# A mixture of experts' second product for both column halves ahead of most outputs

## The chip, the cores and the metric

The kernel runs on one core of a Trainium2 chip. That core has five engines with instruction streams of their own: PE (TensorE, matrix products; its weight loads are shown as PEld), DVE (VectorE), ACT (ScalarE), POOL (GpSimd) and SP (SyncE, which here issues all transfers). Sixteen transfer engines (DMA) move data between the chip's memory and the core. The metric is the device time of one execution, in microseconds (us). The kernel before takes 621.01 us, the median of three runs (620.48 to 622.41).

## The reference

Attention with a learned bias, whose output is the input x of a soft mixture of experts. Batch B = 8, 8 heads, sequence 576, head size 64; so x has 8 x 576 = 4608 rows of 512. There are 8 experts with 4 slots each (32 slots) and a hidden size of 1024. The expert part is:

```python
logits = x @ phi                                   # 4608 x 32
d = softmax over the rows of logits
slot_input = d.T @ x                               # 32 x 512
for e in range(8):
    h = np.maximum(slot_input[e] @ w1[e], 0.0)     # 4 x 1024
    slot_out[e] = h @ w2[e]                        # 4 x 512
c = softmax over the slots of logits               # 4608 x 32, the combine weights
return c @ slot_out                                # 4608 x 512
```

The matrices w1 and w2 have 512 x 1024 and 1024 x 512 numbers per expert, in fp32. All that follows from `slot_input` on needs every row of x, as the first softmax runs over all rows.

## The kernel before

**The long part.** Some 545 of the 620 us go to attention, in 32 units of two heads and one batch, and to the logits and slot inputs of the batches. Its order is written out by hand, in the table `END` (line 42) and in `PLAIN`, and it ends at line 820. The change leaves it as it is. Behind line 820 the order on each engine is chosen by a planner that goes by the order of the program text as priority, puts later work that is ready by its own estimates into an engine's gaps, and adds all waits. Each engine then runs its list strictly in that order.

**Weights.** `fetch_w` (line 755) loads one tile of 512 KB per call: 32 tiles of w1, then 32 of w2, in the list `worder` (line 745). A tile of w2 is one expert, half of the hidden size (`fq`) and half of the 512 output columns (`hf`). The list goes by column half first: 16 tiles of column half 0, then 16 of column half 1, and within a half by expert group `Q` (four experts each), `fq`, and expert `g`. 41 of the 64 tiles are asked for in the hand-ordered part, into every buffer that comes free there; the others follow in the loop of the first product (lines 862 to 884), each into the buffer of a w1 tile that the loop has used, and two behind it (line 886). All of them go through SP's queue.

**First product.** The loop over j = 0 to 7 (lines 862 to 884) takes expert group Q = j // 4 and a quarter kc of the 512 inputs. The eight matmuls of one j put four experts side by side on PE (L867). After four j the result passes a ReLU on ACT into `hS2[Q]` (L881). `turn_hidden(Q)` (line 854) turns these rows with 8 PE transposes (L858) and two copies into `hT2[Q]`, as the second product needs them. Both calls use PSUM tile 3.

**Turned combine weights.** `stack(b)` (line 835) prepares batch b's combine weights for the last matmul: DVE splits them into a rounded part and its remainder (L839, L840), PE turns both (five transposes, L844 and L845, in PSUM tile 2), and ACT or DVE copies 128 x 576 numbers into `cst` (line 846). One `stack` stands in each of the eight turns of the loop.

**Second product.** Lines 893 to 939 run once per column half `hf`. The 64 matmuls of a half (L900, two instructions each in the trace) sum over the hidden size for both expert groups. The loop goes over `Q`, `fq`, then a quarter `x` of the tile, and innermost over the four experts' tiles `g`. DVE and ACT copy the sums to `so` (L905); two matmuls with the selection matrices `sel` fold the experts' rows together (L908); ACT and DVE write `sst`, again a rounded part and its remainder (L910, L911).

**Outputs.** For each of eight batches, four matmuls (L930) give 512 rows of 256 columns; two copies of 128 x 512 (`ld.copy`, lines 114 and 120) bring them to a buffer `ob`, and one transfer of 512 KB stores it in rows of 4 KB (L933). The last 64 of the 576 rows take one more matmul per batch (L936) and a copy per two batches into `obr`, stored for four batches at once, 256 KB in pieces of 1 KB from 64 partitions (L939). `ld.copy` (line 109) chooses ACT or DVE by a running estimate of their load. `ps(k)` is a PSUM tile of two banks, with k = 0 to 3; a new use of one waits for the last one's end.

Of the kernel before, what the change touches and what calls it, by code (L numbers as in the profile page):

```python
# [10 lines left out]
F32 = mybir.dt.float32  # L11
F32R = mybir.dt.float32r
AF = mybir.ActivationFunctionType
ALU = mybir.AluOpType
# [111 lines left out]
def body(ctx, tc, qk, v, wcol, phi, mw1, mw2, tabh, consth, out):  # L126
    nc = tc.nc
    P = 128
    S, D = 576, 64
    B, NP = qk.shape[0:2]  # L130
    H = 2 * NP
    NSL = phi.shape[1]
    E, DM, F = mw1.shape
# [6 lines left out]
    wp = ctx.enter_context(tc.tile_pool(name="wp", bufs=W1N))  # L140
    ldp = ctx.enter_context(tc.tile_pool(name="ldp", bufs=2))
    bsp = ctx.enter_context(tc.tile_pool(name="bsp", bufs=5))
    yp = ctx.enter_context(tc.tile_pool(name="yp", bufs=4))
    atp = ctx.enter_context(tc.tile_pool(name="atp", bufs=1))
    xp = ctx.enter_context(tc.tile_pool(name="xp", bufs=1))
    smp = ctx.enter_context(tc.tile_pool(name="smp", bufs=4))

    ld = Split(nc)

    def ps(k):  # L150

        return psp.tile([P, 2, 512], F32, name="ps", tag=f"r{k}")
# [165 lines left out]
    for i, x in enumerate(END.split()):  # L318
        n, u = x.rstrip("+").split("/")
# [490 lines left out]
    homes = {21: (bsp, "bm"), 22: (ldp, "qk"), 27: (ldp, "qk"), 32: (atp, "at0"), 34: (atp, "at1"), 36: (xp, "xk")}  # L810
# [21 lines left out]
        nc.vector.tensor_scalar(out=sel[Q], in0=rsum, scalar1=rowm[:, Q:Q + 1], scalar2=None, op0=ALU.mult)  # L832
    csts = [bsp.tile([P, S], F32R, name="cst", tag="br", bufs=1)]

    def stack(b):
        cst = csts[b]
        cs = xp.tile([P, 5, 2, 2, 32], F32R, name="cs", tag=("acc", "et")[b % 2])
        ckb = ck[:, b].unsqueeze(2).to_broadcast([P, 5, 2, 32])
        nc.vector.tensor_copy(out=cs[:, :, :, 0, :], in_=ckb)  # L839
        nc.vector.tensor_tensor(out=cs[:, :, :, 1, :], in0=ckb, in1=cs[:, :, :, 0, :].bitcast(F32), op=ALU.subtract)  # L840
        csf = cs.bitcast(F32).rearrange("a c x y s -> a c (x y s)")
        pt = ps(2).rearrange("a x n -> a (x n)")
        for c in range(4):
            nc.tensor.transpose(out=pt[:, c * P:(c + 1) * P], in_=csf[:, c, :], identity=ident)  # L844
        nc.tensor.transpose(out=pt[:, 512:576], in_=csf[0:64, 4, :], identity=ident[0:64, 0:64])  # L845
        ld.copy(cst, pt[:, 0:576], 576)
# [3 lines left out]
    def hidden():  # L850
        hS2.append(wp.tile([P, 2, 512], F32, name="hS", tag="w"))
        hT2.append(wp.tile([P, 8, P], F32, name="hT", tag="w"))

    def turn_hidden(Q):
        pt = ps(3)
        for z in range(2):
            for x in range(4):
                nc.tensor.transpose(out=pt[:, z, x * P:(x + 1) * P], in_=hS2[Q][:, z, x * P:(x + 1) * P], identity=ident)  # L858
            ld.copy(hT2[Q][:, 4 * z:4 * z + 4, :], pt[:, z].rearrange("a (x n) -> a x n", x=4), 512)

    ph = None
    for j in range(8):
        Q, kc = j // 4, j % 4
        ph = ps(Q) if kc == 0 else ph
        for n in range(2):
            for g in range(4):
                nc.tensor.matmul(ph[32 * g:32 * g + 32, n, :], sT[:, kc, :], wtiles[4 * j + g][n],  # L867
                                 start=kc == 0, stop=kc == 3, tile_position=(0, 32 * g))

        if j == 0:  # L870
            csts.append(wp.tile([P, S], F32R, name="cst", tag="w"))
        elif j in (1, 2):
            csts += [wp.tile([P, S], F32R, name="cst", tag="w") for _ in range(2)]
        elif j in (3, 4):
            csts.append(wp.tile([P, S], F32R, name="cst", tag="w"))
            hidden()
        for i in range(4 * j + (1, 2, 2, 3, 3, 0, 0, 0)[j], 4 * j + 4):
            if nw[0] < len(worder):
                fetch_w(homeof[i])
        if kc == 3:  # L880
            nc.scalar.activation(out=hS2[Q], in_=ph, func=AF.Relu, scale=stS)  # L881
        if j == 4:
            turn_hidden(0)
        stack(j)
    turn_hidden(1)
    while nw[0] < len(worder):
        fetch_w((wp, "w"))
    wi = 32


    so = wp.tile([P, 2, 512], F32, name="so", tag="w")
    sstt = wp.tile([P, DM], F32R, name="sst", tag="w")
    for hf in range(2):
        ds = slice(256 * hf, 256 * hf + 256)
        po = ps(3)[:, 0].rearrange("a (x n) -> a x n", x=2)
        for Q in range(2):
            for fq in range(2):
                for x in range(4):
                    for g in range(4):
                        nc.tensor.matmul(po[32 * g:32 * g + 32, Q, :], hT2[Q][:, 4 * fq + x, 32 * g:32 * g + 32],  # L900
                                         wtiles[wi + g][x // 2][:, 256 * (x % 2):256 * (x % 2) + 256], start=fq == 0 and x == 0,
                                         stop=fq == 1 and x == 3, tile_position=(0, 32 * g))
                wi += 4
        for Q in range(2):
            (nc.scalar.copy if Q else nc.vector.tensor_copy)(out=so[:, hf, 256 * Q:256 * Q + 256], in_=po[:, Q, :])  # L905
        pf = ps(2)[:, 0]
        for Q in range(2):
            nc.tensor.matmul(pf[:, 0:256], sel[Q], so[:, hf, 256 * Q:256 * Q + 256], start=Q == 0, stop=Q == 1)  # L908
        sst = sstt[:, ds]
        nc.scalar.copy(out=sst, in_=pf[:, 0:256])  # L910
        nc.vector.tensor_tensor(out=sst[64:], in0=pf[64:, 0:256], in1=sst[64:].bitcast(F32), op=ALU.subtract)  # L911
        ld.act = ld.dve = 0.0
        for bq in range(2):
            obr = wp.tile([P, 4, 256], F32, name="obr", tag="w")
            for i in range(4):
                b = 4 * bq + i
                cst = csts[b]
                if hf == 1:
                    ob = (yp, bsp)[bq].tile([P, 4, 256], F32, name="ob", tag=("y", "bm")[bq])
                elif b > 3:  # L920
                    ob = wp.tile([P, 4, 256], F32, name="ob", tag="w")
                elif b % 2 == 0:
                    pool, tag = ((atp, "at0"), (xp, "xk"))[b // 2]
                    obs = pool.tile([P, 2, 4, 256], F32, name="ob", tag=tag)
                    ob = obs[:, 0]
                else:
                    ob = obs[:, 1]
                po = ps(b % 2).rearrange("a x (y n) -> a (x y) n", y=2)
                for c in range(4):
                    nc.tensor.matmul(po[:, c, :], cst[:, c * P:(c + 1) * P], sst, start=True, stop=True)  # L930
                for z in range(2):
                    ld.copy(ob[:, 2 * z:2 * z + 2, :], po[:, 2 * z:2 * z + 2, :], 512)
                nc.sync.dma_start(out=out[b, hf, :, 0:1024], in_=ob.rearrange("p c d -> p (c d)"))  # L933
                if i % 2 == 0:
                    pr = ps(2).rearrange("a x (y n) -> a (x y) n", y=2)
                nc.tensor.matmul(pr[0:64, i % 2, :], cst[:, 512:576], sst, start=True, stop=True)  # L936
                if i % 2 == 1:
                    ld.copy(obr[0:64, i - 1:i + 1, :], pr[0:64, 0:2], 512)
            nc.sync.dma_start(out=out[4 * bq:4 * bq + 4, hf, 0:64, 1024:1280].rearrange("b p d -> p b d"), in_=obr[0:64])  # L939


def _tables():
# [54 lines left out]
```

## Time and profile before

| | |
|---|---|
| median of three runs | 621.01 us (620.48 to 622.41) |
| profiled execution | 621.36 us, its span 619.6 us |
| busy: PE, DVE, ACT, POOL | 95%, 68%, 77%, 36% of the span |
| transfers | 110.72 MB, mean 179 GB/s |
| L867, first product | 128 instructions, 548.6 to 569.8 us |
| L900, second product | 256 instructions, first from 575.2, last from 598.6 us |
| L933 and L939, outputs | 20 issues, from 588.1 to 613.2 us; 9.44 MB |

All times within the execution count from the start of the span. An engine's busy share is an average over stages that have different limits, so the part around the change has to be read on its own. In the views of time windows, the columns are busy us of PE, PEld, DVE, ACT and POOL with the number of instructions, the mean granted TensorE clock (1.00 is full speed), the mean busy share of the transfer engines (overlapping packets can bring it above 1) and GB/s.

### The profile page before, as it was taken

How to read it: one execution, taken by the hardware profiler on the slowest of the kernel's cores; microseconds unless marked ns; L12 is line 12 of the kernel's file. 1: busy time of each engine (PE TensorE's matmuls, PEld its weight loads, DVE VectorE, ACT ScalarE, POOL GpSimd, SP SyncE). 2: the span in 40 equal slices, each digit the busy share in tenths (PEclk: the TensorE clock that was granted, in tenths of full speed). 3: DMA queues.
4: the chain of work that ended last, by engine and by line, in shares of the span. 5: the costliest groups of instructions: out<-in, count | busy, mean ns of one | idle time of the engine just before them, and what ended most of it. 6: DMA issues, size and time to landing. Idle time of an engine off the chain costs nothing.

```text
span 619.6 us, 18796 instructions
## 1 busy us (share of the span) xinstructions
PE 591.4 (95%) x7359; PEld 378.6 (61%) x7359; DVE 422.6 (68%) x1339; ACT 474.0 (77%) x979; POOL 223.9 (36%) x336
## 2 busy tenths in 40 slices
PE   6998899999999999999999999999999999999882
PEld 3764566666666666666666666666656666544452
DVE  7997766666666766666667666686788887664143
ACT  6997788888888888888888888787886877532242
POOL 0001544545554445455544454444423334000000
PEclk9999899999999999999999999999999999999897
DMA  6768223224854453494334458323123326999988
GB/s 215 277 234 291 61 83 105 99 87 141 252 195 153 150 182 125 157 278 160 115 116 121 149 210 282 107 84 115 46 82 122 118 91 221 322 332 349 312 306 306
DMA packets 54568, 110.72 MB, mean 179 GB/s; under 512 B 7120, under 2 KB 24656, under 8 KB 54480
## 3 DMA queue, kind: packets, MB, share of 16 engines
q1 hardware_dynamic: 54480, 109.52, 53.4%
q8 instruction: 58, 0.95, 0.7%
q14 instruction: 30, 0.25, 0.1%
HBM read 82.10 MB, written 27.41 MB: 177 GB/s over the span
## 4 chain that ended last, share of the span: by engine, by line
PE 86%; DVE 4%; ACT 4%; DMA 3%; issue 1%; SPq 0%; POOL 0%; ACTq 0%; DVEq 0%; POOLq 0%
PE ps L471 26%; PE ps L368 21%; PE ps L346 17%; PE ps L364 5%; PE ps L258 4%; PE ps L900 3%; PE ps L867 3%; PE ps L537 1%; PE ps L930 1%; PE ps L667 1%; ACT e L262 1%; ACT y L388 1%; DMA bias_m<-e 1%; DVE f L237 1%; DMA bias_r<-e 1%
## 5 line engine op out<-in xcount | busy, mean ns | idle before, releaser
L310 POOL TENSOR_SCALAR y<-y,sm 128x576 f32<-128x576 f32 (+1 forms) x320 | 221.0, 703 | 305.2 <-DVE sm L397 250.4
L381 DVE CUSTOM_DVE_ANT_0 y<-ps,bm 128x576 f32<-128x576 f32 x256 | 185.2, 754 | 97.6 <-PE ps L346 58.3
L388 ACT ACTIVATE y<-y,mn 128x576 f32<-128x576 f32 x288 | 222.1, 772 | 29.2 <-DVE sm L396 18.0
L313 ACT COPY at<-ps 128x1024 f32<-128x1024 f32 (+3 forms) x211 | 153.9, 732 | 37.5 <-PE ps L346 28.3
L471 PE MATMUL ps<-at,v 128*64 128x320 f32 (+1 forms) x1280 | 176.1, 414 | 0.0
L368 PE MATMUL ps<-qk 64*128 64x288 f32 x1024 | 157.1, 423 | 0.8 <-DVE mn L381 0.8
L346 PEld LDWEIGHTS ps<-ident,y 64*128 64x128 f32 x2624 | 104.9, 139 | 54.6 <-POOL y L310 15.5
L346 PE MATMUL ps<-ident,y 64*128 64x64 f32 x2624 | 118.9, 226 | 4.0 <-POOL y L310 3.6
L471 PEld LDWEIGHTS ps<-at,v 128*64 128x64 f32 x1280 | 84.0, 137 | 60.4 <-issue 10.6
L368 PEld LDWEIGHTS ps<-qk 64*128 64x128 f32 x1024 | 93.6, 188 | 25.6 <-DVE sm L396 10.8
L388 ACT ACTIVATION_READ_ACCUMULATOR y<-y,mn 128x1 f32 x288 | 54.0, 188 | 0.0
L258 PE MATMUL ps<-f,wbd 128*32 128x79 f32 (+32 forms) x856 | 47.7, 345 | 2.9 <-DVE f L237 2.4
L237 DVE TENSOR_SCALAR f<-tabs,scl,nb 128x576 f32<-128x576 f32 (+17 forms) x114 | 47.9, 496 | 0.9 <-DMA tabs<-in_tab_dram 0.9
L313 DVE COPY at<-ps 128x256 f32<-128x256 f32 (+3 forms) x77 | 33.7, 441 | 17.2 <-PE ps L346 13.0
L258 PEld LDWEIGHTS ps<-f,wbd 128*32 128x32 f32 x856 | 29.6, 112 | 20.9 <-issue 10.0
L364 PE MATMUL ps<-qk 64*64 64x288 f32 x256 | 38.0, 415 | 0.0
L313 DVE COPY xts<-ps 128x256 f32<-128x256 f32 (+1 forms) x57 | 25.9, 454 | 9.2 <-PE ps L471 6.2
L262 ACT ACTIVATE e<-ps,bcon 128x591 f32<-128x591 f32 x36 | 26.5, 751 | 5.2 <-DMA bias_m<-e 2.8
L397 DVE RECIPROCAL sm<-sm 128x2 f32<-128x2 f32 (+1 forms) x160 | 26.7, 167 | 5.5
L396 DVE TENSOR_SCALAR sm<-sm 128x2 f32<-128x2 f32 (+1 forms) x160 | 27.8, 174 | 2.8 <-ACT y L388 2.4
L381 DVE CUSTOM_DVE_ANT_0 y<-ps,br 128x576 f32<-128x576 f32 x32 | 23.9, 748 | 2.5 <-DMA br<-bias_r 1.0
L381 DVE DVE_READ_ACCUMULATOR2_ANT mn<- 128x1 f32 x288 | 23.9, 83 | 0.0
(147 smaller groups left out, 366.9 us busy)
## 6 DMA issues: line engine op xcount, KB each, us to landing
wt<-in_moe_w_dram SPq DMA_DIRECT2D x63, 512.0 KB, 6.1
qk<-in_qk_dram SPq DMA_DIRECT2D x32, 608.0 KB, 3.8
v<-in_v_dram SPq DMA_DIRECT2D x32, 320.0 KB, 3.1
bias_m<-e SPq DMA_DIRECT2D x32, 295.5 KB, 4.0
out_dram<-ob SPq DMA_DIRECT2D x16, 512.0 KB, 4.5
xs<-xts SPq DMA_DIRECT2D x24, 288.0 KB, 5.6
xo<-xs SPq DMA_DIRECT2D x8, 864.0 KB, 5.9
bm<-bias_m SPq DMA_DIRECT2D x16, 288.0 KB, 3.9
```

The costliest lines, as they stand in the source:

```text
L237: nc.vector.tensor_scalar(out=f, in0=tabs[:, 0:n], scalar1=scl[:, sc:sc + 1], scalar2=nb1[:, 0:1], op0=ALU.mult, op1=ALU.max)
L258: nc.tensor.matmul(pb[32 * t:32 * t + 32, c0 // 512, c0 % 512:(c1 - 1) % 512 + 1], wbd, x, start=True, stop=True, tile_position=(0, 32 * t))
L262: nc.scalar.activation(out=e, in_=pb.rearrange("a x n -> a (x n)")[:, 0:S + 15], func=AF.Identity, bias=bc)
L310: nc.gpsimd.tensor_scalar(out=out, in0=y, scalar1=r, scalar2=1.0, op0=ALU.mult, op1=ALU.mult)
L313: (nc.vector.tensor_copy if eng else nc.scalar.copy)(out=out, in_=in_)
L346: nc.tensor.matmul(out, src[rs], ident[rs, rs], is_transpose=True, start=True, stop=True, tile_position=(64 * r, 0))
L364: nc.tensor.matmul(pss[0].t[rs, n, 0:HALF], x[rs, 1152:1216], x[rs, 64 + n * HALF:64 + (n + 1) * HALF], start=True, stop=True, tile_positi ...
L368: nc.tensor.matmul(pss[hh].t[:, n, 0:HALF], x[rs, 640 + p * P:640 + (p + 1) * P], x[rs, k0:k0 + HALF], start=True, stop=True, tile_positio ...
L381: nc.vector.tensor_tensor_reduce(out=d["y", p][:, hs].rearrange("a (x n) -> a x n", x=2), in0=t[:, :, 0:HALF], in1=biases[hp][p][:, hs].re ...
L388: nc.scalar.activation(out=y, in_=y, func=AF.Exp, bias=d["mn", p][:, hh:hh + 1], scale=-1.0, accum_out=d["sm", p][:, hh:hh + 1])
L396: nc.vector.tensor_scalar(out=r, in0=r, scalar1=1e-9, scalar2=None, op0=ALU.add)
L471: nc.tensor.matmul(po[64 * hh:64 * hh + 64], d["v"][:, v0:v0 + 64], main[:, :, 4 * hh + i, :] if i < 4 else rest, start=i == 0, stop=i == ...
```

## The change

The loop of the first product keeps only the turn of batch 0. The second product, its fold and `sst` become a function `second(hf)`, and `turn_hidden(1)`, in PSUM tile 2, moves between the two expert groups of `second(0)`. Then come the outputs of batches 0 and 1 for column half 0, with the turns of batches 1 and 2; then `second(1)`; then the same two batches' outputs for column half 1. The other six batches are written whole: one matmul covers all 512 columns, a copy moves 1024 columns, and a transfer of 512 KB holds 256 rows in pieces of 2 KB. Each turns the next batch's combine weights, in PSUM tile 3. Last rows are stored for two batches at a time and one column half per transfer, 128 KB each. The buffers of the outputs come from a list, `homes`. In all there are 16 transfers of 512 KB and 8 of 128 KB, in place of 16 and 4 of 256 KB.

```diff
-    def stack(b):
+    def stack(b, k=2):
...
-        pt = ps(2).rearrange("a x n -> a (x n)")
+        pt = ps(k).rearrange("a x n -> a (x n)")
...
     def turn_hidden(Q):
-        pt = ps(3)
+        pt = ps(3 - Q)
...
         if j == 4:
             turn_hidden(0)
-        stack(j)
-    turn_hidden(1)
+        if j == 0:
+            stack(0)
...
+    homes = [(atp, "at0")] * 2 + [(xp, "xk")] * 2 + [(wp, "w")] * 4 + [(yp, "y")] * 4 + [(bsp, "bm")] * 4
+    spare = []
+
+    def place():
+        pool, tag = homes.pop(0)
+        if spare:
+            return spare.pop()
+        if tag not in ("at0", "xk"):
+            return pool.tile([P, 2, 2, 256], F32, name="ob", tag=tag)
+        x = pool.tile([P, 2, 2, 2, 256], F32, name="ob", tag=tag)
+        spare.append(x[:, 1])
+        return x[:, 0]
+
+    def second(hf):
+        nonlocal wi
+        po = ps(3)[:, hf].rearrange("a (x n) -> a x n", x=2)
         for Q in range(2):
+            if hf == 0 and Q == 1:
+                turn_hidden(1)
             for fq in range(2):
                 for x in range(4):
                     for g in range(4):
...
+        ds = slice(256 * hf, 256 * hf + 256)
+        nc.scalar.copy(out=sst[:, ds], in_=pf[:, 0:256])
+        nc.vector.tensor_tensor(out=sst[64:, ds], in0=pf[64:, 0:256], in1=sst[64:, ds].bitcast(F32), op=ALU.subtract)
+
+    def outputs(b, hf):
+
+        cst, ob = csts[b], place()
+        ds = slice(256 * hf, 256 * hf + 256)
+        po = ps(b % 2).rearrange("a x (y n) -> a x y n", y=2)
+        for c in range(4):
+            nc.tensor.matmul(po[:, c // 2, c % 2, :], cst[:, c * P:(c + 1) * P], sst[:, ds], start=True, stop=True)
+        for z in range(2):
+            ld.copy(ob[:, z], po[:, z], 512)
+        nc.sync.dma_start(out=out[b, hf, :, 0:1024], in_=ob.rearrange("p x y d -> p (x y d)"))
+
+    def last_rows(b, ds):
+
+        n = ds.stop - ds.start
+        obr = wp.tile([P, 2, n], F32, name="obr", tag="w")
+        for i in range(2):
+            pr = ps(2)[0:64, 0, 0:n]
+            nc.tensor.matmul(pr, csts[b + i][:, 512:576], sst[:, ds], start=True, stop=True)
+            ld.copy(obr[0:64, i], pr, n)
+        for hf in range(ds.start // 256, ds.stop // 256):
+            o = 256 * hf - ds.start
+            nc.sync.dma_start(out=out[b:b + 2, hf, 0:64, 1024:1280].rearrange("b p d -> p b d"), in_=obr[0:64, :, o:o + 256])
+
+    second(0)
+    ld.act = ld.dve = 0.0
+    for b in range(2):
+        if b > 0:
+            stack(b)
+        outputs(b, 0)
+    last_rows(0, slice(0, 256))
+    stack(2)
+    second(1)
+    for b in range(2):
+        outputs(b, 1)
+    last_rows(0, slice(256, 512))
+    for b in range(2, B):
+        cst = csts[b]
+        for z in range(2):
+            ob = place()
+            po = ps(z)
+            for c in range(2):
+                nc.tensor.matmul(po[:, c, :], cst[:, (2 * z + c) * P:(2 * z + c + 1) * P], sst, start=True, stop=True)
+            ld.copy(ob.rearrange("p h c d -> p c h d"), po.rearrange("p c (h d) -> p c h d", h=2), 1024)
+            nc.sync.dma_start(out=out[b, :, :, 512 * z:512 * z + 512].rearrange("h p d -> p h d"),
+                              in_=ob.rearrange("p h c d -> p h (c d)"))
+        if b + 1 < B:
+            stack(b + 1, 3)
+        if b % 2:
+            last_rows(b - 1, slice(0, 512))
```

More of the change, by code (lines that the diff above doesn't have):

```diff
@@ L891, in body @@
     so = wp.tile([P, 2, 512], F32, name="so", tag="w")
[L892 to L895, printed above, removed]
+    sst = wp.tile([P, DM], F32R, name="sst", tag="w")
+    homes = [(atp, "at0")] * 2 + [(xp, "xk")] * 2 + [(wp, "w")] * 4 + [(yp, "y")] * 4 + [(bsp, "bm")] * 4
[12 more added lines that the diff above has]
+        po = ps(3)[:, hf].rearrange("a (x n) -> a x n", x=2)
         for Q in range(2):
+            if hf == 0 and Q == 1:
+                turn_hidden(1)
             for fq in range(2):
@@ L908, in body @@
             nc.tensor.matmul(pf[:, 0:256], sel[Q], so[:, hf, 256 * Q:256 * Q + 256], start=Q == 0, stop=Q == 1)
[L909 to L939, printed above, removed]
```

## The prediction

> **What bounds the kernel now.** I read the page's 40 slices first, to see where a limit other than the matrix engine holds.
>
> ```profile
> span 619.6 us, 18796 instructions
> ...
> DMA  6768223224854453494334458323123326999988
> GB/s 215 277 234 291 61 83 105 99 87 141 252 195 153 150 182 125 157 278 160 115 116 121 149 210 282 107 84 115 46 82 122 118 91 221 322 332 349 312 306 306
> ```
>
> A slice is 15.5 us. Over the last seven (the weights and outputs of the expert stage, all that the change touches) the transfers are busy 80 to 99%. So I cut that stage by the transfers' state (busy time of each engine, granted TensorE clock, share of the transfer engines, GB/s):
>
> ```profile
> 548.00:586.00 38.00, 34.80 (x328) 15.01 (x327) 12.06 (x27) 7.69 (x13) 0.00 (x0) 0.96 1.09 347
> 586.50:589.00 2.50, 2.50 (x29) 1.73 (x28) 1.29 (x2) 1.65 (x3) 0.00 (x0) 1.00 0.27 92
> 589.00:601.50 12.50, 11.08 (x133) 6.79 (x131) 5.40 (x9) 5.12 (x10) 0.00 (x0) 1.00 0.98 363
> 601.50:604.50 3.00, 2.21 (x16) 1.95 (x17) 1.29 (x2) 1.65 (x3) 0.00 (x0) 1.00 0.18 53
> 604.50:617.50 13.00, 4.16 (x26) 3.00 (x24) 4.54 (x7) 4.33 (x8) 0.00 (x0) 0.77 0.99 361
> ```
>
> The expert weights fill the transfer engines until 586, the first column half's outputs from 589 to 601.5, the second half's from 604.5 to 617.5. The two holes are what can be won: 2.5 x 0.73 + 3.0 x 0.82 = 4.3 us idle. What the first hole waits for stands in the transfer issues on SP, and where it and the second come from in the chain of waits (start, us, what):
>
> ```profile
> 544.52 36.77 SPq L778 DMA_DIRECT2D wt<-in_moe_w_dram  x27
> 588.07 3.62 SPq L933 DMA_DIRECT2D out_dram<-ob  x4
> ```
>
> ```profile
> 550.49 0.59 PE ps L844 x4
> 551.08 0.20 PE ps L845
> ...
> 559.99 2.71 PE ps L867 x24
> ...
> 572.31 0.67 PE ps L858 x4
> ...
> 575.18 8.21 PE ps L900 x128
> ...
> 587.40 1.00 PE ps L900 x16
> ...
> 594.94 4.05 PE ps L900 x70
> 599.01 0.44 DVE so L905
> ...
> 601.06 0.44 DVE sst L911
> ...
> 603.00 0.70 DVE ob L120
> ```
>
> First hole: the first half's product (L900, 128 instructions for its 64 fp32 matmuls) starts at 575.18 and is followed by the same tail as the second, so its first output is issued at 588.07, just when the weights run out. Second hole: PE runs the second half's product in the gaps between outputs (the row at 587.40) and its last 70 instructions from 594.94. It ends at 599.0; fold, outputs and issue follow, and the first half's queued outputs drain before the second's arrive.
>
> Two instants are needed more exactly, the landing of the last weights and the first bytes of the second half's outputs:
>
> ```profile
> 587.50:588.00 0.50, 0.50 (x12) 0.26 (x8) 0.50 (x2) 0.50 (x2) 0.00 (x0) 1.00 0.19 64
> 588.00:588.50 0.50, 0.50 (x9) 0.17 (x2) 0.50 (x2) 0.38 (x1) 0.00 (x0) 1.00 0.03 10
> ...
> 604.00:604.50 0.50, 0.50 (x6) 0.50 (x6) 0.29 (x1) 0.00 (x0) 0.00 (x0) 1.00 0.00 0
> ...
> 617.50:618.00 0.50, 0.00 (x0) 0.00 (x0) 0.00 (x0) 0.00 (x0) 0.00 (x0) 0.50 0.27 72
> ```
>
> The last weights land at about 588.1, the second half's bytes start at 604.5, which is 5.5 us after the product's last matmul, and the last bytes leave at 617.7.
>
> **The change, part by part.**
>
> *Earlier start of the first product.* Seven of the eight turns of combine weights leave the first product's loop. One costs PE 0.59 + 0.20 = 0.79 us, so 5.5 us. The loop is then 128 L867 instructions at 2.71/24 = 0.113 us, 14.5 us from 548.6, with one turn and the first turn of hidden rows (1.3 us) to 564.4. Half of the second product's first column half follows (8.21/2 = 4.1 us) and hides the ReLU of the second half of the hidden rows; turning those takes what it takes now, 572.31 to 575.18 = 2.9 us; then 4.1 us more. It ends near 575.5 instead of 583.4. The fold and two batches' outputs need 4.7 us (599.0 to 603.7), so the first output is ready near 580.5.
>
> *What that buys.* SP issues weights until 544.52 + 36.77 = 581.3, and they occupy the transfer engines until 588.1. The early outputs (two of 512 KB, one of 128 KB, 1.18 MB) queue behind them. They fill the first hole, and no more: at 361 GB/s they last 3.3 us. SP issues 24 output transfers in place of 20; four take it 3.62 us (the row at 588.07), 0.9 each, less than the 1.4 us that 512 KB move in, so its queue costs nothing. The weights themselves don't come sooner: the engines are at 1.09 busy over 548 to 586, so PE freeing buffers earlier only lengthens the queue.
>
> *The second product now waits for the last weights.* Its last quarter (32 instructions, L900) reads the last four weight tiles. These land 0.524 MB / 347 GB/s = 1.5 us apart. The loop goes over the four tiles innermost, so all but about six instructions wait for the last tile: 26 after 588.1. At full clock one costs 4.05/70 = 0.058 us, so 1.5 us. But PE, behind in-order waits, does nearly nothing from 584 to 588: three bursts of two to four matmuls. Here is what the clock does after a slack window, with two starts of weight loads in the slow one:
>
> ```profile
> 570.50:573.90 3.40, 1.84 (x12) 1.23 (x12) 0.76 (x1) 2.24 (x3) 0.00 (x0) 1.00 1.10 349
> 573.90:577.30 3.40, 2.73 (x24) 1.20 (x26) 0.00 (x0) 0.58 (x1) 0.00 (x0) 0.51 1.10 348
> ...
> 604.70:608.10 3.40, 2.49 (x17) 1.73 (x15) 2.77 (x5) 1.79 (x4) 0.00 (x0) 1.00 0.99 394
> ```
>
> ```profile
> 575.61 0.20 PEld L900 LDWEIGHTS ps<-wt,hT 128*32 128x32 f32 x4 [0.23 <-issue]
> 576.04 0.20 PEld L900 LDWEIGHTS ps<-wt,hT 128*32 128x32 f32 x4 [0.23 <-issue]
> ```
>
> PE was busy 1.84 of 3.4 us (54%) and the granted clock fell to 0.51 for the next 3.4; at 2.49 of 3.4 (73%) it stayed at 1.00. In the slow window four instructions take 0.43 us, 0.107 each, so the 26 take 2.8 us. The wait before them has PE busy for at most a third, nearer to the first row: I take 2.8 us and keep 1.5 as the lower end. The skill weighs the other way: the Trainium skill, "TensorE: Matmul & The Clock Gate", section "What's actually happening", has the clock halve after an idle window of about 3.4 us; as the bursts leave no gap over 1.5 us, a literal reading keeps the clock up and gives 1.5 us. The first row already shows a window that was not idle followed by a halved clock.
>
> *Fold and first output.* Same instructions as now, 5.5 us from last matmul to first bytes. They sit on the path, since only 1.18 MB of output can cover them.
>
> *Whole outputs of six batches.* Each column-half pair becomes two copies of 1024 columns in place of four of 512, and a turn runs beside them:
>
> ```profile
> L114 ACT COPY ob<-ps 128x512 f32<-128x512 f32 x18 | 10.1, 588 | 9.5 <-DVE ob L120 4.2 <-PE ps L930 3.9 <-issue 1.4
> L313 ACT COPY at<-ps 128x1024 f32<-128x1024 f32 x120 | 121.3, 1012 | 31.9 <-PE ps L346 23.2
> L313 DVE COPY at<-ps 128x1024 f32<-128x1024 f32 x8 | 9.7, 1215 | 0.6 <-PE ps L346 0.6
> L839 DVE CAST cs<-ck 128x320 fp32r<-128x320 f32 x8 | 3.8, 479 | 6.6 <-PE ps L845 6.6
> L840 DVE TENSOR_TENSOR cs<-ck,cs 128x320 fp32r<-128x320 f32 x8 | 3.9, 487 | 0.2
> L120 DVE CAST cst<-ps 128x576 fp32r<-128x576 f32 x4 | 3.0, 755 | 6.3 <-PE ps L845 6.3
> ```
>
> A batch costs ACT and DVE about 1.01 + 1.22 for outputs, 0.48 + 0.49 + 0.76 for the turn and 0.6 for its last rows (a 512-column copy), 4.6 us over two engines, 2.3 us. Its 1.18 MB take 3.3 us to move. So these copies and the moved turns are hidden by the transfers; were that cover gone, six turns would cost at most 6 x 1.7/2 = 5 us. Where one turn waits, the next batch's matmuls are behind it, and there is 1 us of slack per batch, growing.
>
> The output pieces shrink from 4 KB to 2 KB a row. The nearest rows are the 2.3 KB rows written early in the kernel:
>
> ```profile
> 51.00:53.00 2.00, 2.00 (x32) 0.89 (x31) 1.78 (x4) 0.85 (x2) 0.00 (x0) 1.00 1.03 405
> ...
> 610.30:611.50 1.20, 0.74 (x4) 0.53 (x4) 0.28 (x1) 0.58 (x2) 0.00 (x0) 1.00 0.97 182
> 611.50:616.30 4.80, 0.00 (x0) 0.00 (x0) 0.41 (x1) 0.58 (x1) 0.00 (x0) 0.50 1.01 410
> ```
>
> They move at 405 GB/s, the 4 KB rows at 410: nothing, at most 0.3 us over 6.3 MB. The last rows (64 partitions, 1 KB pieces) move at 182 GB/s in either kernel; as there are more and smaller ones, their slow stretch may overlap better (a rival below).
>
> **Sum**, in the profiled execution: 588.1 (last weights) + 2.8 (rest of the product, slow clock) + 5.5 (fold, first output, first bytes) + the remaining 9.44 - 1.18 = 8.26 MB at 361 GB/s, 22.9 = 619.3, against 617.7 now: **1.6 us more**. One hole of about 5 us replaces two of 4.3 in all, and it sits behind a PE that has been waiting. The profiled execution took 621.36 us, 0.35 over the median of 621.01; added to the median this is **622.6 us**.
>
> **Rivals.**
>
> *Clock stays up.* Sum 588.1 + 1.5 + 5.5 + 22.9 = 618.0, 0.3 more: 621.3 us. For it: the turns and early outputs may fall into the wait and keep PE busier, or the planner may leave other work there. Against it: the 570.50 row.
>
> *Thin transfers overlap (faster).* Now a 256 KB last-rows transfer takes 0.262/182 = 1.44 us against 0.64 at 410 GB/s; seven eighths of four of them remain after the hole, up to 3.5 x 0.8 = 2.8 us if the smaller ones hide entirely between full ones. With the slow clock that is 1.2 us below now, 619.8 us; with the full one 2.5 below, 618.5. Only with both, or most of both, is it faster beyond 0.3%. For it: smaller pieces in a full queue. Against it: in the 610.30 row full outputs stood in the queue too, and the share was 0.97.
>
> *Cover lost (slower).* Instructions run in order on PE, and the planner fills gaps with the second product (row at 587.40). If it puts the last quarter ahead of an early output or its last rows, these wait for 588.1 as well and cover nothing: up to 3.3 us more, 625.9 us; it decides as soon as one early output stands behind the last tile. For it: now such fillers stand between every two batches. Against it: about 7 us lie between the early outputs' readiness and 588.
>
> *Not what it says.* The planner may order PE so that the halves interleave as now; then the holes stay as they are, 621.0 us.
>
> **Chances.** Forecast 0.40, clock up 0.18, thin transfers 0.22, cover lost 0.16, not what it says 0.04. A measurement of this kernel tells about 0.3%, 1.9 us, from no change. The forecast's +1.6 lies just inside it; with half a microsecond or more of error on either side I put 0.23 of its 0.40 inside and 0.17 over. Clock up: 0.17 inside, 0.01 over. Thin transfers: 0.16 faster, 0.06 inside. Cover lost: 0.14 slower, 0.02 inside. No effect: inside. Together faster 0.16, same 0.52, slower 0.32. The forecast's own range is 621.0 to 623.6 (full clock and early landing; or fold at slow clock too, 0.6, and landing 0.4 late). The whole range, 618.8 to 625.6, takes in the thin transfers with most of the clock, and a cover nearly lost.
>
> **What would show it.** Right: one hole instead of two, beginning near 591 and 4 to 6 us wide; the first output issued near 581 on SP; L900 finishing near 591; clock 0.50 just before; transfers at about 360 GB/s with no gap from 596 to 619. Wrong: weights landing earlier than 588, last rows at well over 182 GB/s, output gaps after 597 (the copies or turns bind), or an early output issued after 588.

## The result, and the profile after

The changed kernel takes 624.59 us, the median of eight runs (623.03 to 627.45); the kernel before took 620.99 us beside it. The ratio is 1.0055, with a 95% interval of 1.0032 to 1.0078: slower by about half a per cent, 3.4 us. The time lies in the whole range of the prediction (618.8 to 625.6), above the forecast's own (621.0 to 623.6), and 2.0 us over its point. The likeliest of its three cases, no change that can be told, did not come; the case "slower", at 0.32, did.

The profiled execution took 623.99 us. Its page, the span and the 40 slices of transfers:

```profile
span 621.8 us, 18721 instructions
...
DMA  6778123234844554593344369223213346999968
GB/s 215 276 233 303 46 90 115 81 107 133 274 160 149 176 163 121 171 296 120 115 123 149 116 228 301 67 82 120 64 58 121 121 153 209 330 334 348 321 227 305
```

A slice is now 15.55 us. Of the last three, the middle one (590.7 to 606.3) has fallen to 60% busy and 227 GB/s. The same windows as before the change, cut by the state of the transfers (busy us of PE, PEld, DVE, ACT, POOL; clock; share; GB/s):

```profile
548.00:585.50 37.50, 35.49 (x399) 15.89 (x391) 8.66 (x19) 7.03 (x12) 0.00 (x0) 1.00 1.08 347
585.50:588.00 2.50, 1.53 (x12) 0.28 (x4) 0.00 (x0) 0.00 (x0) 0.00 (x0) 1.00 1.05 406
588.00:591.00 3.00, 1.92 (x27) 0.90 (x26) 0.29 (x1) 0.00 (x0) 0.00 (x0) 1.00 0.35 130
591.00:596.00 5.00, 3.91 (x22) 2.91 (x23) 2.59 (x7) 2.40 (x5) 0.00 (x0) 1.00 0.00 0
596.00:620.30 24.30, 12.52 (x49) 7.75 (x48) 11.61 (x14) 10.22 (x14) 0.00 (x0) 0.82 0.98 340
```

One hole has taken the place of two. It holds 3.0 x 0.65 + 5.0 = 7.0 us of idle transfers, where the two held 4.3. Next to nothing moves from 591 to 596. These are the first and the last half microsecond of the stretch that began at 596:

```profile
596.00:596.50 0.50, 0.50 (x3) 0.16 (x2) 0.50 (x1) 0.36 (x1) 0.00 (x0) 1.00 1.05 426
...
620.00:620.50 0.50, 0.00 (x0) 0.00 (x0) 0.00 (x0) 0.00 (x0) 0.00 (x0) 0.50 0.12 37
```

What the hole waits for is one unbroken run in the chain of waits (start, us, what):

```profile
579.60 9.12 DMA wt<-in_moe_w_dram
...
588.76 1.93 PE ps L916 x26
590.71 0.44 DVE so L921
...
591.19 1.15 PE ps L924 x4
592.36 0.38 ACT sst L926
592.76 0.44 DVE sst L927
...
593.25 0.75 PE ps L935 x4
...
594.07 1.08 ACT ob L114 x2
```

In the changed kernel L916 is the second product, L921 the copies to `so`, L924 the fold, L926 and L927 write `sst`, and L935 are the outputs of one column half. PE stands still for the last weight tile, which is reported at 588.72; then 26 instructions of the product, the fold, `sst`, the first output and its copies follow one another, and nothing that could be stored is left. The early outputs themselves were ready in time. On SP their first issue is at 581.0:

```profile
L938 SPq DMA_DIRECT2D out_dram<-ob x4: 332/360/2273, 581.0 to 595.8; - x4
```

One thing must be allowed for when profiles are compared. The hand-ordered part, which the change doesn't touch, ended 0.9 us sooner in this execution: the first product's first instruction started at 547.7 in place of 548.6, and the profiled times are 2.6 us apart where the medians are 3.6 apart. The weights did not land sooner for it: the report of the last tile stands at 588.72 here, and in the landing records of the trace before at 588.68. The start of the first product:

```profile
L867 PE MATMUL ps<-wt,sT x128: 592/592/617, 547.7 to 563.6; 128*32 128x512 f32 x128
```

### The profile page after: what moved, and what is told of

Same layout as the page of the kernel before. It is cut to its first block, busy times and chain, and to the rows that moved or that the text cites. A ratio compares the mean times of both kernels' runs of the same rounds, so it can differ in the third digit from the quotient of the medians.

```text
span 621.8 us, 18721 instructions
## 1 busy us (share of the span) xinstructions
PE 591.8 (95%) x7329; PEld 376.7 (61%) x7329; DVE 422.3 (68%) x1334; ACT 473.6 (76%) x974; POOL 223.6 (36%) x336
## 4 chain that ended last, share of the span: by engine, by line
PE 86%; DMA 4%; ACT 3%; DVE 3%; issue 1%; SPq 1%; POOL 0%; ACTq 0%; DVEq 0%; POOLq 0%
PE ps L471 26%; PE ps L368 21%; PE ps L346 17%; PE ps L258 6%; PE ps L364 5%; PE ps L867 2%; PE ps L916 2%; DMA wt<-in_moe_w_dram 1%; PE ps L537 1%; PE ps L667 1%; ACT y L388 1%; PE ps L970 1%; DMA bias_m<-e 1%; DMA out_dram<-ob 1%; DMA bias_r<-e 1%
## 5 line engine op out<-in xcount | busy, mean ns | idle before, releaser
L258 PE MATMUL ps<-f,wbd 128*32 128x79 f32 (+31 forms) x856 | 47.7, 345 | 2.8 <-DVE f L237 2.2
```

What stands on the lines that cost most here:

```text
L258: nc.tensor.matmul(pb[32 * t:32 * t + 32, c0 // 512, c0 % 512:(c1 - 1) % 512 + 1], wbd, x, start=True, stop=True, tile_position=(0, 32 * t))
```

## The experiments

Theory A: the time is set by the one hole, which opens between the last weights and the first bytes of the second half, and which only output written ahead can cover. Against it stood: B, the smaller pieces of the whole outputs and the split last rows; C, a halved clock after PE's wait; D, the turns between the early outputs; E, that the order chosen by the planner, or the making of the outputs, sets the pace. Ratios are to the kernel before, run beside each on the same chip.

**None, four or eight batches ahead.** Three kernels that differ from the change only in the number of batches whose half 0 is written ahead of `second(1)`:

```diff
-    for b in range(2):
+    for b in range(0):        # range(4), range(8) in the others
         if b > 0:
             stack(b)
         outputs(b, 0)
...
-    for b in range(2, B):
+    for b in range(0, B):     # range(4, B); with eight none is left
```

> No batch's outputs of the first column half ahead of the second product (the change has two batches); everything else as in the change. Theory A (one hole, between the last weights and the second half's first outputs, covered only by the 1.18 MB written ahead): nothing covers it, the hole opens near 589 and lasts about 7 us, 3.3 us more work stays behind it: the time rises by about 3.3 us over the change, to 627.9 us. Theory B (the slower time comes from the whole outputs in 2 KB pieces and the split last rows): about two thirds of a microsecond more for two more batches in that form, 625 us. Theory C (the product after the wait runs at half clock in most executions): as the change, 624.6, or a little over.

Measured: 628.27 us (627.32 to 628.96), ratio 1.0135 (1.0111 to 1.0159). Windows of that kernel:

```profile
585.40:588.80 3.40, 1.65 (x7) 0.27 (x4) 0.00 (x0) 0.00 (x0) 0.00 (x0) 1.00 0.72 231
...
590.00:592.00 2.00, 2.00 (x24) 0.90 (x17) 0.00 (x0) 0.00 (x0) 0.00 (x0) 0.50 0.00 0
...
589.00:598.00 9.00, 7.60 (x48) 4.43 (x48) 3.20 (x6) 3.04 (x5) 0.00 (x0) 0.82 0.01 2
598.00:600.00 2.00, 1.52 (x9) 0.96 (x8) 2.00 (x4) 1.05 (x2) 0.00 (x0) 1.00 0.95 360
```

The transfers stand still for nine microseconds, where A asked for about seven; B and C both expected less than 626 us. Here PE was busy for 49% of 3.4 us, and the clock did fall to 0.50 for the product's last 26 instructions. They took 3.26 us by the chain of waits, against 1.93 in the change.

> Four batches' outputs of the first column half ahead of the second product instead of two; the other four whole. Theory A: 1.18 MB more stand in the hole, which shrinks from 5 us to about 1.7: 3.3 us less than the change, 621.3 us; the last rows of batches 2 and 3 stand behind the last weight tile on PE, so 0.7 us of this may be lost. Theory B: a third of the whole outputs are gone, 1.2 us less, 623.4 us. Theory C: PE has more to do in the wait and stays at full clock; 1.3 us less at most, 623.3 us.

Measured: 620.85 us (619.43 to 623.09), ratio 1.0002 (0.9977 to 1.0027). Its windows:

```profile
585.00:592.00 7.00, 6.90 (x74) 3.49 (x72) 3.55 (x7) 2.29 (x5) 0.00 (x0) 1.00 1.02 382
592.00:597.00 5.00, 3.72 (x23) 2.94 (x23) 3.68 (x8) 2.35 (x5) 0.00 (x0) 1.00 0.08 32
597.00:617.40 20.40, 8.57 (x39) 5.10 (x36) 7.93 (x9) 8.26 (x14) 0.00 (x0) 0.78 1.00 347
```

So 628.27, 624.59 and 620.85 with none, two and four batches ahead: 3.7 us for every two by the medians, near the 3.3 us in which their 1.18 MB move at 361 GB/s. The ratios to the kernel before, which was run beside each, put the steps at 5.0 and 3.3 us, each uncertain by about 2 us; the slow clock above is part of the first. This is A's cover, measured to that accuracy, and B (623.4) and C (623.3) missed here too. The hole is still 5 us wide; four batches fill the wait ahead of it as well.

> All eight batches' outputs of the first column half ahead of those of the second in the text, none whole (pieces of 4 KB), last rows for two batches and one half at a time. Theory A: no hole; the transfers run from the weights to the end, 5.1 us less than the change and 0.6 less for 4 KB pieces: about 618.5 us, below the kernel before. Theory B: only the split last rows are left of its cause, about 621.5 us. Theory C: 623.3 us.

Measured: 628.51 us, ratio 1.014 (1.0119 to 1.0162). All theories missed. Windows and a stretch of the chain of this kernel:

```profile
588.00:596.00 8.00, 6.33 (x61) 3.57 (x59) 4.67 (x10) 3.41 (x8) 0.00 (x0) 1.00 0.74 289
596.00:612.00 16.00, 11.35 (x39) 8.12 (x40) 4.63 (x8) 4.20 (x9) 0.00 (x0) 0.51 0.33 122
```

```profile
596.67 1.11 PE ps L844 x4
597.79 0.31 PE ps L845
...
598.12 0.77 DVE cst L120
...
598.93 1.22 PE ps L935 x4
600.15 0.85 PE ps L844 x4
...
605.24 0.79 PE ps L924
```

From 596 the outputs are made one after another: turn (L844, L845), copy to `cst`, output, next turn, at half clock, at 122 GB/s. The fold starts only at 605.24, behind the outputs of all eight batches, although the weights have long been there. In this order more output ahead helps only while PE can make it, turns included, before the last weights land.

**4 KB rows for the six batches.** The change, with the six batches written per column half in place of whole:

```diff
-        cst = csts[b]
-        for z in range(2):
-            ob = place()
...
+        outputs(b, 0)
+        outputs(b, 1)
```

> The change with the six later batches written by column halves in rows of 4 KB (two copies of 512 and one transfer per half) instead of whole in pieces of 2 KB; order, turns and last rows as in the change. Theory A: the hole of 5 us stays; only the rate returns from 393 to 410 GB/s over 6.3 MB, 0.6 us: 624.0 us. Theory B: back to the kernel before, 621 to 622 us. Theory C: 624.6 us.

Measured: 625.42 us (624.85 to 628.59), ratio 1.01 (1.0067 to 1.0133). B, which hoped for 621 to 622, falls: the larger pieces gained nothing on the whole. Its profiled execution, at 628.59 us, says why the clock belongs in the sum:

```profile
588.20:591.60 3.40, 1.46 (x12) 0.43 (x12) 0.00 (x0) 0.00 (x0) 0.00 (x0) 1.00 1.00 383
...
591.40:594.80 3.40, 3.38 (x26) 1.39 (x26) 0.00 (x0) 0.00 (x0) 0.00 (x0) 0.53 0.19 69
...
607.00:608.00 1.00, 0.75 (x6) 0.75 (x7) 0.78 (x2) 0.15 (x1) 0.00 (x0) 1.00 0.62 246
612.00:613.00 1.00, 1.00 (x10) 1.00 (x9) 0.00 (x0) 0.95 (x3) 0.00 (x0) 1.00 0.06 21
```

PE was busy for 43% of the wait, and the 26 instructions after it ran at 0.53. In the last stretch the transfers now run dry at 607 and 612: with twice the matmuls and copies beside the turns, the outputs come too slowly. So what the larger pieces could gain in the moving was lost in the making. By its time alone this run does not isolate what the pieces cost; the packet records of its trace do, below.

**Turns back in the loop.** Seven of the eight turns return to the first product's loop, where the kernel before had all eight:

```diff
-        if j == 0:
-            stack(0)
+        if j < 7:
+            stack(j)
```

> The change with seven of the eight turns of combine weights back in the first product's loop (the last batch's is still turned one ahead); order of products and outputs as in the change. Theory A (the one hole sets the time): the second product of column half 0 ends some 5 us later, its outputs are ready near 585, still before the weights' end; the hole is the same: 624.6 us, at most 0.5 less. Theory D (the turns between the whole outputs slow the last stretch of transfers, 24.2 us in the change where 22.9 were expected): 1.3 us less, 623.3 us.

Measured: 624.24 us (623.32 to 627.94), ratio 1.0069 (1.0043 to 1.0095). D falls for the most part: the last stretch of transfers, 596.9 to 620.7 in this trace, took 23.8 us, against 24.2 in the change and the 22.9 that D asked for. The times alone could not tell, as the two intervals leave about 2 us either way. The turns cost the change little where they stand, as the prediction had it. Then the same with eight and with six batches ahead:

> Seven turns back in the loop, and all eight batches' outputs of column half 0 ahead of those of half 1 in the text, rows of 4 KB, last rows for two batches at a time. Theory A with D (the kernel with all eight ahead failed because a turn between every two outputs held them to 7 us per two batches, against 3.3 that they take to move): with the turns done before, the outputs come at about 2.4 us per two batches, there is no hole, transfers run from the weights to the end: 617 us, 4 below the kernel before. Theory E (it failed because the planner puts the second half's fold behind all of the first half's outputs): still above 624 us.

Measured: 619.49 us (618.02 to 621.97), ratio 0.9975 (0.9956 to 0.9995), 9 us less than with the turns between the outputs. The turns are all in which the two kernels differ, so they held up the one with all ahead (its half clock came with them: in this stage there is none here before 611). But it stopped 2.5 us short of what A and D expected:

```profile
592.00:599.00 7.00, 6.45 (x76) 3.25 (x68) 1.63 (x4) 1.53 (x4) 0.00 (x0) 1.00 0.99 373
599.00:603.00 4.00, 2.27 (x15) 1.83 (x16) 1.72 (x3) 2.11 (x6) 0.00 (x0) 1.00 0.11 41
```

```profile
595.03 2.32 PE ps L916 x38
...
597.85 1.15 PE ps L924 x4
...
602.96 0.59 ACT ob L114
```

PE reaches the product's last 38 instructions only at 595.03, behind the outputs, and the same tail opens a hole of 4 us at a later place.

> As the one with seven turns in the loop, with six batches' outputs of column half 0 ahead and two batches written whole. Theory A with D: 3.5 MB of cover against a wait of 7.3 us from the last weights to the second half's first bytes, so no hole or half a microsecond of one; 617 to 618 us. Theory E: near 621 us or above.

Measured: 619.42 us (618.37 to 620.28), ratio 0.998 (0.9967 to 0.9994). The same, with its hole from 594.4 to 598.4: PE itself, with 70 instructions of the product after 588.66, was late here, and no longer the weights.

**Four turns in the loop, four batches ahead.**

> Four turns in the loop (those of the four batches ahead), four batches' outputs of column half 0 ahead, the other four turned one batch ahead and written whole. Against the kernel with four ahead and all turns late (620.85 us, where the second half's outputs restarted 1.2 us later than in the change because turns and last rows stood before the fold): theory A with D gives those 1.2 us back, 619.6 us. Theory E: the same, 620.9 us.

Measured: 620.00 us (619.44 to 621.24), ratio 0.9988 (0.9972 to 1.0003), between what A and D expected (619.6) and what E did (620.9), and not told apart from either, nor from no change.

**The fold among outputs of the first half.** If A were all, the hole would close once there is something to store while the fold runs. Here `second(1)` stands between the half 0 outputs of two groups of batches, all of half 1 comes last, and seven turns are in the loop:

```diff
     second(0)
-    for b in range(2):
+    for b in range(4):        # range(6) in the second kernel
         outputs(b, 0)
...
     second(1)
+    for b in range(4, B):
+        outputs(b, 0)
...
-    for b in range(2):
+    for b in range(B):
         outputs(b, 1)
```

> Seven turns of combine weights in the first product's loop; then the second product of column half 0, half 0's outputs of four batches, the second product of half 1, half 0's outputs of the other four batches, and only then all outputs of half 1 (4 KB rows throughout, last rows for two batches and one half). Theory A (one hole, which opens because nothing that is ready may be written between the last weights and the first bytes of the second half, and which is closed by output of the first half that is written there): the four batches ahead last until about 592 as in the run with four ahead; the product ends at 591 to 592, the next first-half outputs follow it on PE at once, so transfers pause for 1.5 to 2 us at most instead of 5.2, and the fold's 5.5 us lie beside the 6.5 us of transfers of the four remaining first-half batches. Against the run with four ahead (620.85, transfers ending at 617.4) some 3.5 us less: 617.0 to 617.8 us. Theory E (the planner's order or the making of the outputs, not their place in the text, limits the stretch): PE has to do product, fold and outputs one after the other as before, and the time stays at 619.4 to 620.8 us.

> As the other kernel of this call, but six batches of half 0 ahead of the second product of half 1 and two behind it. Theory A: as in the run with six ahead and whole outputs the product ends near 592.7, later than the weights, since the outputs' turns stand before it; the two batches behind it give 3.3 us of transfers against a tail of 5.5 us, of which the six batches' queue covers about 1.5, so a pause of 1 to 1.5 us stays instead of 4: 616.8 to 617.8 us. Theory E: 619.4 us as there.

Measured: 620.23 us (617.51 to 626.02), ratio 0.9988 (0.9962 to 1.0014), with four ahead; 619.27 us (618.04 to 619.96), ratio 0.997 (0.9951 to 0.9989), with six. Both are what E expected. Windows and chain of the first of them:

```profile
591.30:594.00 2.70, 2.57 (x16) 1.96 (x15) 1.63 (x3) 1.82 (x4) 0.00 (x0) 1.00 0.20 77
594.00:596.50 2.50, 1.04 (x5) 0.65 (x6) 1.15 (x3) 1.17 (x3) 0.00 (x0) 1.00 1.00 405
596.50:600.00 3.50, 2.90 (x20) 2.17 (x19) 1.78 (x4) 1.71 (x4) 0.00 (x0) 1.00 0.60 205
```

```profile
591.88 0.45 PE ps L924 x2
592.33 0.36 PE ps L935 x3
...
592.72 0.59 ACT ob L114
...
593.34 0.55 DVE ob L120
...
594.91 0.38 ACT obr L114
...
596.12 0.66 PE ps L844 x4
```

The hole of 5 us has become one of 2.7 us at 20% and one of 3.5 us at 60%, 3.6 us idle in all. Each output passes PE, ACT and DVE in turn, and last rows, fold and the one late turn stand between them in PE's order; the transfers empty faster than this chain fills them. The second kernel has its hole from 596 to 601; there ACT also waited 0.9 us for an output buffer (`ob`) whose earlier transfer had not landed. It is the fastest of those that store everything, 0.3% below before; its interval ends 0.1% below it, and it is the best of ten, so part of the 0.3% may be chance.

**What last rows cost.** The two last kernels compute the last rows but leave out storing some: in the changed kernel those of batches 2 to 7 (six transfers of 128 KB), in the kernel before those of column half 1 (two of 256 KB).

```diff
-            last_rows(b - 1, slice(0, 512))
+            last_rows(b - 1, slice(0, 512), False)   # no transfer
```

> The changed kernel with the last rows of batches 2 to 7 computed and copied as before, but never stored: these rows of the output are left out. Six transfers of 128 KB, 0.79 MB, are missing from the last stretch. If they cost what their bytes do at 393 GB/s, the rate of the 2 KB rows: 2.0 us less than the changed kernel, 622.6 us. If they cost what the profile shows in the stretches they hold (182 to 227 GB/s, 0.79 MB at 200: 3.9 us): 620.7 us. The rival of thin transfers that overlap says the former for this kernel and the latter for the kernel before.

> The kernel before with the last rows of column half 1 computed and copied but never stored: these rows of the output are left out. Two transfers of 256 KB, 0.52 MB, are missing from the last stretch, after both holes. By bytes at 410 GB/s: 1.3 us less than before, 619.7 us. By the 182 GB/s of the stretch they hold: 2.9 us less, 618.1 us.

Measured: 620.84 us, ratio 0.9986 (0.9964 to 1.0008), and 618.16 us, ratio 0.9953 (0.9934 to 0.9972). Against the change's 1.0055 the first saves 0.69%, 4.3 us, for 0.79 MB; the second saves 0.47%, 2.9 us, for 0.52 MB. That is 182 GB/s in both, as in the prediction's row at 610.30. That the three agree so closely is luck: the intervals leave the first saving uncertain by about 2 us and the second by 1.2 us. Both still lie above the price by bytes (2.0 and 1.3 us), so thin transfers cost more than their bytes in either kernel. Without them, in the changed kernel, the stretch from first to last byte is

```profile
595.70:615.60 19.90, 11.02 (x49) 6.88 (x48) 11.63 (x14) 10.22 (x14) 0.00 (x0) 0.94 1.01 375
```

at 375 GB/s, the 0.13 MB of last rows of batches 0 and 1 still among them.

## Why the prediction was right or wrong

**Right: the structure.** One hole instead of two, from 591, 5 us wide (4 to 6 forecast); first output issued at 581.0 (near 581); the product done at 590.69 (near 591). That the hole is what counts, and that output ahead is its only cover, is shown by none, two and four ahead. One sign did not come: the clock stood at 1.00 before the hole, not at 0.50.

**The sum, term by term**, in the profiled execution:

| term | predicted | measured |
|---|---|---|
| last weights | 588.1 | 588.72 |
| rest of the product | 2.8 | 1.93 |
| fold, first output, first bytes | 5.5 | 5.3 |
| remaining 8.26 MB | 22.9 | 24.2 |
| last bytes | 619.3 | 620.2 |

*Where it failed:* the step "the remaining 8.26 MB at 361 GB/s, 22.9". It took the mean rate of the old last stretch, which had the same ninth of thin transfers in it, and put the smaller pieces at "nothing, at most 0.3 us". From 596.0 to 620.2 the bytes moved at 341 GB/s, 1.3 us longer. The runs without most last rows allow a cut. In the changed kernel 7.47 MB took 19.9 us; less 0.13 MB of thin rows at 182 GB/s, 0.7 us, the full outputs ran at 7.34/19.2 = 382 GB/s. In the kernel before without the last rows of column half 1, its 4.19 MB left between the first byte, 604.4, and 615.1:

```profile
604.40:615.10 10.70, 4.18 (x27) 3.01 (x24) 4.54 (x7) 4.32 (x8) 0.00 (x0) 0.86 0.98 392
```

Over 7.34 MB the difference makes 0.5 us. These rates hold pauses as well. The traces also record every packet with its size and duration, and those separate the pieces. In the changed kernel's last stretch a packet of 2 KB took 86.7 ns in the mean, which is 378 GB/s for 16 engines. A packet of 4 KB took 164.1 ns in the last stretch of the kernel before (399 GB/s) and 163.2 ns in the kernel with 4 KB halves (401). Over the 6.29 MB in 2 KB pieces that makes 0.9 us, three times what I allowed. So the smaller pieces were the larger part of the 1.3 us, and the kernel with 4 KB halves did move its packets faster; it lost that by running dry. Another 0.2 us is a reading: 361 GB/s is the rate up to 617.5, while the old stretch ended at 617.7, which makes 358. The last 0.2 us is not separated.

*Landing*, 0.6 too early: I read the last weights off the rate of the bytes, at 588.1. PE goes by the report of the transfer, at 588.72, which comes after the bytes. The kernel with none ahead shows it without output in between: its bytes end by 589.0, and PE's wait ends at 589.46.

*Slow clock*, 0.9 too much in this execution: the clock held at 1.00. The clock records of the traces show why. They know two values, 1.00 and 0.50, and between the first and the last change a value always lasts a whole multiple of 3.413 us (3.41, 34.13 and 501.76 us in the trace before). So the clock changes only at the edges of a grid of such windows. Counted back from the change at 597.79, the changed kernel's windows are:

```profile
584.14:587.55 3.41, 2.44 (x35) 1.02 (x28) 1.04 (x3) 0.00 (x0) 0.00 (x0) 1.00 1.08 386
587.55:590.97 3.42, 2.37 (x28) 0.90 (x26) 0.26 (x1) 0.00 (x0) 0.00 (x0) 1.00 0.44 167
...
594.38:597.79 3.41, 2.00 (x8) 0.86 (x6) 2.24 (x3) 2.88 (x6) 0.00 (x0) 1.00 0.53 214
597.79:601.21 3.42, 2.97 (x9) 2.15 (x9) 1.23 (x1) 1.25 (x2) 0.00 (x0) 0.50 0.99 322
```

An edge, at 587.55, fell into PE's wait for the weights, so that work before and after it filled the two windows to 72% and 69%. Laid on the wait alone, 585.41 to 588.82, a window would have had 50%. In the kernel with none ahead exactly that stretch was a window of the grid, busy for 48%, and the clock fell at its end; in the kernel with 4 KB halves the window that ended at 591.59 had 43%, and it fell too. So the forecast's mechanism is real, but the windows lie differently in each execution, and that the rival "clock stays up" had this term is luck. The clock did fall later in the same execution, at 597.79, behind the hole. The Trainium skill, "TensorE: Matmul & The Clock Gate", section "What's actually happening", lets the clock halve after an idle window; the windows here that were half busy and still halved it are not covered by that, and the measurement decides.

*Executions and medians.* The untouched part before 548 ended 0.9 us sooner in the profiled execution after, and no term had that; as the weights landed no sooner, it changed none of the terms above. The sum misses its last bytes by 0.9, but the kernel's median by 2.0. The rest is how single executions stand to their medians: that of before lay 0.35 above, and I took the one after to lie so too; it lay 0.6 below.

**Edits costed at nothing.** The moved turns: right as far as can be told, the time with seven of them back in the loop is the same within 0.3%. They cost about 9 us, however, once eight batches are to be written ahead. SP's queue: the 24 issues nowhere ended a wait in the hole.

**Rivals.** *Thin transfers overlap* fell: leaving out 0.79 MB of them saved 4.3 us, not 2.0. *Cover lost* did not occur: the early outputs were issued from 581.0 on, ahead of the wait. *Not what it says* fell with the single hole. *Clock stays up* held for its own term, not for its time.

**The chances.** Forecast +1.6 us and a bound of 1.9 left 0.3 us of room, and I gave "within 0.3%" 0.52. The terms that were read too low, last stretch and landing, make 1.9 us together, and the clock gave back 0.9. A forecast that near to the bound had its two sides about equally likely, and the bounds of the last stretch should have been wider than 0.3 us.

## What to carry to other kernels

When a load is the last thing to land, count what can still be written after it until its result is ready: each microsecond of the chain behind the load that no ready output covers is lost, and 1.18 MB of output written ahead was worth 3 to 5 us here. Putting more ahead pays only while the engines can make it before the load lands; past that point the making, not the moving, sets the end, and turns that cost little elsewhere cost about 9 us. Price a last stretch by its parts, thin transfers and full ones at their own rates, and not by a mean taken from other sizes.

## What was not expected

- Early output did not wait for the last weight to land. The 16 transfer engines finished the last tile at different times, from 585.93 to 588.72 by the landing records, and those that had finished went on with output. From 585.5 to 588 the rate rose from the 347 GB/s of weights alone to 406; by the packet records 0.77 of the 1.01 MB moved then were output in packets of 4 KB, which alone run at about 400, and the rest weights in packets of 1 KB. So no gain from the mixture as such is shown. At most 130 GB/s x 3.0 us = 0.39 MB of the 1.18 MB of early output was left after 588.
- The clock falls after windows in which PE is far from idle, but the busy share alone does not decide it. From 60 us on, over the grids of all 14 traces, every window at full clock that was busy for less than 44% was followed by half clock, and none that was busy for 67% or more. In between both happened: 59% before the change at 597.79 above, while 65% in the kernel before (597.84 to 601.26) left the clock at 1.00.
- Last rows cost the same per byte in transfers of 128 KB and of 256 KB as far as the times without them can tell. Their pieces of 1 KB are not the whole cause: the weights came in packets of 1 KB as well, at 51 ns each in the kernel before, where a packet of last rows took 74 ns. Whether the 64 partitions or the direction make the difference, no run separates.
- No order of the same work came more than 0.3% below the kernel before: the hole moved from place to place (591 to 596, 592 to 597, 594 to 598, 596 to 601, 599 to 603) and shrank below 4 us only where making the outputs then left others.
